# Block inverse by interleaved independent streams on VectorE, and GpSimd limited to one-input operations, in a DeltaNet and Soft-MoE kernel

**Chip, cores, metric.** One core of a Trainium2 chip. The time is the device time of a run in microseconds (us). Ratios are the mean time of one kernel's fast runs over that of the kernel before in the same rounds, so not quite the ratio of the medians that stand beside them. Below, PE is TensorE, DVE VectorE, ACT ScalarE, POOL GpSimd, SP SyncE.

## The reference, cut to what matters

```python
def _attn_ref(q, k, v, beta):                 # (4, 8, 768, 48) each; beta (4, 8, 768)
    k_n = k / (np.linalg.norm(k, axis=-1, keepdims=True) + 1e-06)
    for t in range(S):
        y[:, :, t] = einsum(q_t, state)
        v_old = einsum(state, k_n_t)
        state = state + beta_t * outer(k_n_t, v_t - v_old)
# x = y as (3072, 384); logits = x @ phi (32 slots); softmax over tokens -> slot_input = d.T @ x
# 8 experts: relu(slot_input @ w1) @ w2; softmax over slots -> out = c @ slot_out
```

The kernel works in 24 chunks of 32 tokens, six groups of four. In a chunk the recurrence becomes a product with the inverse of a triangular 32x32 matrix for each of the 32 (batch, head) pairs. The 128 inverses of a group's four chunks are computed at once, one per partition.

## The kernel before

While group n runs, VectorE eliminates the inverses of group n+1, a few steps at a time, in program order between its other work. Each step is a product and then a subtraction of that product:

```python
        def eliminate(j):                                   # 31 of them per group
            m, w = j + 1, C - 1 - j
            ...
            nc.vector.tensor_tensor(prv, tt[:, j, 0:m]..., lb[:, j, j + 1:C]..., op=ALU.mult)
            nc.vector.tensor_tensor(tt[:, j + 1:C, 0:m], tt[:, j + 1:C, 0:m], prv, op=ALU.subtract)
```

GpSimd does three two-input products per chunk on 128 partitions (and the scalings of `lb` and of the inverse):

```python
    def scale_v(cc):
        nc.gpsimd.tensor_tensor(Vt[cc], Vt[cc], nT[n][...].broadcast_to([P, U, D]), op=ALU.mult)
    def weights(cc):
        nc.gpsimd.tensor_tensor(Ab[cc % NT], wide(GQ[n][:, c, :, :, 1, :]...), tri..., op=ALU.mult)
        nc.gpsimd.tensor_tensor(Tb[cc % NT], wide(TT[n][:, c * U:(c + 1) * U, :]), own..., op=ALU.mult)
```

The dependence that matters: `R = V - K S` is a VectorE operation, and TensorE's solve (`T R`, 32 products) waits for it:

```python
        def rest():
            state(0, ks)                                    # TensorE: K S into PSUM
            nc.vector.tensor_tensor(R, Vt.pop(cc), ks, op=ALU.subtract)
        def solve():                                        # 32 matmuls: lhsT=T[y][:, u], rhs=R
        ...
        # order in a chunk
        hook("head"); drain(EL[c][0]); rest(); read(); scale_v(x + 2); ...; drain(EL[c][1])
        solve(); turn(...); ...; drain(EL[c][2]); update(); outputs(); ...; weights(x + 1)
```

`EL[c][p]` are the elimination steps of the next group that are put at place p of chunk c. The group's norms and the scaling of `lb` stand at place 0 of its first chunk, ahead of R.

## Time and profile before

| | before |
|---|---|
| time, median of 3 | 401.38 us |
| profiled span, granted TensorE clock | 398.2 us, 0.843 |
| first solve; groups 0 to 4, solve to solve | 48.9; 54.0, 47.7, 48.6, 45.5, 46.2 us |
| last group and the experts (from solve 20 to the end) | 107.3 us |
| solve idle for R | 31.7 us in 16 waits |

"Solve to solve" is the distance between the first matmuls of two solves in TensorE's timeline. As each chunk needs the state that the one before left, these distances add up to the time of the loop.

### The profile page before, as it was taken

What the parts mean: (1) busy time and instruction counts of PE and PEld (TensorE: products, weight loads), DVE (VectorE), ACT (ScalarE), POOL (GpSimd) and SP (SyncE); (2) the same over time, 40 slices, a digit from 0 to 9 for tenths busy, and PEclk for the clock granted to TensorE, in tenths of its full rate; (3) what the DMA queues carried; (4) which work ended last, traced back from release to release, by engine and by line L of the source; (5) the groups of instructions that cost most, each with busy time, mean ns of one, the idle gap of its engine ahead of it and who ended that gap; (6) DMA issues with size and microseconds to landing.
All of it is one profiled execution on the core that took longest, in us unless ns stands there. A gap on an engine that the chain in (4) does not pass through costs nothing.

```text
span 398.2 us, 16603 instructions
## 1 busy us (share of the span) xinstructions
PE 310.5 (78%) x7391; PEld 247.8 (62%) x7391; DVE 235.4 (59%) x554; ACT 147.8 (37%) x296; POOL 120.5 (30%) x144
## 2 busy tenths in 40 slices
PE   3676869789939897699986898396998968866784
PEld 2555757677938786578775787385986854312243
DVE  6396499651887968689687987979412022101043
ACT  2343223465514564235542463232535521101032
POOL 9320442440504535063350826134352000000000
PEclk9999975996865899758998689856799978999685
DMA  5555445544422245424311011011400499799148
GB/s 96 92 96 82 76 79 86 87 77 67 78 47 38 40 76 113 92 48 98 54 23 22 11 30 29 2 21 21 162 3 4 172 425 426 283 431 428 56 172 302
DMA packets 85031, 45.27 MB, mean 114 GB/s; under 512 B 79424, under 2 KB 82656, under 8 KB 83040
## 3 DMA queue, kind: packets, MB, share of 16 engines
q1 hardware_dynamic: 83296, 43.86, 40.7%
q8 instruction: 58, 0.95, 1.0%
q0 software_dynamic: 576, 0.15, 0.3%
q10 hardware_dynamic: 1088, 0.20, 0.3%
q14 instruction: 13, 0.11, 0.1%
HBM read 39.47 MB, written 4.72 MB: 111 GB/s over the span
## 4 chain that ended last, share of the span: by engine, by line
PE 34%; DVE 26%; SPq 12%; issue 11%; DMA 9%; ACT 3%; POOL 3%; DVEq 0%; POOLq 0%; ACTq 0%
SPq L82 11%; DVE pr L320 10%; DVE tt L323 8%; DMA w2t<-in_moe_w_dram 5%; PE psR L434 5%; PE psS L447 3%; PE pso L879 3%; PE pt L482 3%; PE pt L585 3%; PE pt L211 3%; PE psY L464 3%; DVE R L427 2%; PE psR L420 2%; PE ph L855 2%; PE pt L567 2%
## 5 line engine op out<-in xcount | busy, mean ns | idle before, releaser
L320 DVE TENSOR_TENSOR pr<-tt,lb 128x31 f32<-128x31 f32 (+15 forms) x155 | 76.0, 490 | 7.2 <-POOL lb L312 2.9
L323 DVE TENSOR_TENSOR tt<-tt,pr 128x31 f32<-128x31 f32 (+15 forms) x155 | 70.0, 452 | 5.3
L434 PE MATMUL psR<-R,Tb 64*64 64x48 f32 x768 | 31.4, 238 | 31.7 <-DVE R L427 31.7
L434 PEld LDWEIGHTS psR<-R,Tb 64*64 64x64 f32 x768 | 28.7, 153 | 35.1 <-issue 24.1
L454 ACT ACTIVATE S<-psS 48x768 f32<-48x768 f32 x46 | 37.1, 806 | 30.2 <-PE psS L447 29.9
L312 POOL TENSOR_TENSOR tt<-tt,gm 128x512 f32<-128x512 f32 x10 | 11.4, 1136 | 101.7 <-DVE pr L320 64.8
L396 POOL TENSOR_TENSOR Tb<-TT,own 128x512 f32<-128x512 f32 x24 | 26.4, 1102 | 30.0 <-ACT TT L376 25.3
L240 PE MATMUL pt<-KQ 48*32 48x64 f32 (+1 forms) x1792 | 27.7, 248 | 7.2 <-ACT KQ L227 4.7
L393 POOL TENSOR_TENSOR Ab<-GQ,tri 128x512 f32<-128x512 f32 x24 | 32.1, 1336 | 4.0 <-ACT GQ L244 4.0
L437 ACT ACTIVATE U<-psR 128x384 f32<-128x384 f32 x24 | 11.8, 492 | 57.8 <-PE psR L434 57.8
L464 PE MATMUL psY<-U,Ab 64*64 64x48 f32 x768 | 32.5, 243 | 0.0
L447 PE MATMUL psS<-U,K 32*112 32x96 f32 x736 | 31.1, 321 | 0.7 <-ACT U L437 0.6
L240 PEld LDWEIGHTS pt<-KQ 48*32 48x32 f32 x1792 | 22.4, 124 | 14.4 <-ACT KQ L227 6.1
L464 PEld LDWEIGHTS psY<-U,Ab 64*64 64x64 f32 x768 | 29.2, 157 | 3.0 <-issue 1.2
L244 ACT ACTIVATE GQ<-pt 128x256 f32<-128x256 f32 (+1 forms) x56 | 16.8, 351 | 37.5 <-PE pt L240 37.5
L447 PEld LDWEIGHTS psS<-U,K 32*112 32x112 f32 x736 | 26.8, 223 | 5.5 <-ACT U L437 1.9
L420 PE MATMUL psR<-S,KQ 128*32 128x96 f32 x768 | 26.2, 288 | 1.6 <-issue 1.1
L420 PE MATMUL psY<-S,KQ 128*32 128x96 f32 x768 | 25.2, 283 | 0.0
L385 POOL TENSOR_TENSOR V<-V,nT 128x384 f32<-128x384 f32 x24 | 21.6, 901 | 11.4 <-DMA Q<-in_q_dram 7.5
L269 DVE STREAM_TRANSPOSE lb<-GQ 128x1024 f32<-128x1024 f32 x6 | 11.8, 1968 | 21.0 <-ACT GQ L244 21.0
L211 PE MATMUL pt<-ident,Q 128*128 128x128 f32 x76 | 23.1, 341 | 1.3 <-DMA Q<-in_q_dram 0.9
L420 PEld LDWEIGHTS psR<-S,KQ 128*32 128x32 f32 x768 | 20.3, 129 | 3.8 <-issue 2.1
(143 smaller groups left out, 498.8 us busy)
## 6 DMA issues: line engine op xcount, KB each, us to landing
w2t<-in_moe_w_dram SPq DMA_DIRECT2D x8, 1536.0 KB, 19.0
w1t<-in_moe_w_dram SPq DMA_DIRECT2D x7, 1536.0 KB, 10.6
Q<-in_q_dram SPq DMA_DIRECT2D x96, 48.0 KB, 2.8
V<-in_v_dram SPq DMA_DIRECT2D x96, 48.0 KB, 2.8
out_dram<-ob SPq DMA_DIRECT2D x24, 192.0 KB, 2.4
K<-in_k_dram SPq DMA_DIRECT2D x92, 48.0 KB, 2.5
w1t<-in_moe_w_dram SPq DMA_DIRECT2D x3, 512.0 KB, 4.0
bb<-in_beta_dram POOLq DMA_DIRECT2D x16, 6.0 KB, 2.7
```

The source lines that it names most:

```text
L82: eng.dma_start(out=dst[C * h:C * h + C, :, 0:D], in_=src.rearrange("b (g h) s d -> h s (b g) d", h=4)[h, cc * C:(cc + 1) * C])
L211: nc.tensor.transpose(dst, self.src[a][:, b * G:(b + 1) * G, :].rearrange("p g d -> p (g d)"), ident)
L240: nc.tensor.matmul(pg[g][rh, b], lhsT=kq[r, b, 0, rh], rhs=kq[r, b, a0:a1, rh], start=True, stop=True, skip_group_check=True)
L320: nc.vector.tensor_tensor(prv, tt[:, j, 0:m].unsqueeze(1).broadcast_to([P, w, m]), lb[:, j, j + 1:C].unsqueeze(2).broadcast_to([P, w, m]), ...
L323: nc.vector.tensor_tensor(tt[:, j + 1:C, 0:m], tt[:, j + 1:C, 0:m], prv, op=ALU.subtract)
L393: nc.gpsimd.tensor_tensor(Ab[cc % NT], wide(GQ[n][:, c, :, :, 1, :].rearrange("p b g t -> p (b g) t")), tri.unsqueeze(1).broadcast_to([P, ...
L396: nc.gpsimd.tensor_tensor(Tb[cc % NT], wide(TT[n][:, c * U:(c + 1) * U, :]), own.unsqueeze(1).unsqueeze(3).broadcast_to([P, U, 2, C]), op= ...
L420: nc.tensor.matmul(dst[hs[h], b].rearrange("p g d -> p (g d)"), lhsT=kq[:, b, a, hs[h]], rhs=old[:, h, b, :], start=(b == 0), stop=False, ...
L434: nc.tensor.matmul(pw[half[y], u], lhsT=T[y][:, u], rhs=st["R"][half[y], u], start=(u == 0), stop=True, skip_group_check=True)
L447: nc.tensor.matmul(psS[0:DP + D, h, b * GD:(b + 1) * GD], lhsT=K[hs[h], b * G:(b + 1) * G].rearrange("p g d -> p (g d)")[:, 0:DP + D], rhs ...
L454: nc.scalar.activation(new[r, :, :, g * D:(g + 1) * D], psS[r, :, 0:B * GD].rearrange("p h (b g e) -> p h b g e", b=B, g=G)[:, :, :, g], A ...
L464: nc.tensor.matmul(qs[half[y], b, g], lhsT=at[y][:, u], rhs=st["U"][half[y], u], start=False, stop=True, skip_group_check=True)
```

## The change

Its intent: (1) split the inverse into diagonal blocks (E), a coupling with the lower left block (M) and a combination (L), and interleave their steps so that an operation seldom needs the result of the one directly ahead; (2) no operation on GpSimd with two SBUF inputs, since they hold VectorE's two-input steps (in the profile before, 31 elements took 1.02 us beside such a product, 112 took 0.27 without); (3) the first group's inverse likewise, without TensorE.

```diff
+            for j in range(HC):                      # HC = 16
+                put(..., ea(j)); put(..., ma(j))     # products of streams E and M
+                put(..., es(j)); put(..., ms(j))     # their subtractions
+            for j in range(HC + 1):
+                if j < HC: put(..., la(j))           # products of the combination ...
+                if j > 0:  put(..., ls(j - 1))       # ... one ahead of the sums
     def scale_v(cc):
-        nc.gpsimd.tensor_tensor(Vt[cc], Vt[cc], nT[n]...broadcast_to([P, U, D]), op=ALU.mult)
+        for u in range(U):                           # 8 pieces 128x48
+            nc.gpsimd.tensor_scalar(Vt[cc][:, u], Vt[cc][:, u], nT[n][:, ...], None, op0=ALU.mult)
     def weights(cc):
-        nc.gpsimd.tensor_tensor(Ab[cc % NT], wide(GQ...), tri..., op=ALU.mult)
-        nc.gpsimd.tensor_tensor(Tb[cc % NT], wide(TT...), own..., op=ALU.mult)
+        for h in range(4):                           # 4 pieces 32x256
+            nc.gpsimd.affine_select(out=Ab[...][r, :, h % 2, :], in_=GQ[n][r, c, :, :, 1, :], ...)
+        for h in range(4):                           # 4 pieces 32x256
+            nc.gpsimd.tensor_copy(Tb[...][r, :, h % 2, :], TT[n][r, c * U:(c + 1) * U, :])
-    # scaling of lb, of the inverse, and Call: GpSimd
+    # scaling of lb, of the inverse, and Call: VectorE
-    f0["couple"](0); f0["combine"](0); ...           # first group: half inverse, rest on TensorE
+    drain([t[1] for t in f0["steps"]])               # first group: the same 95 steps
```

The table of what is prepared in chunks 0 to 3 changes with it. The shares of the steps per place stay: .29, .30, .26 and .15 of them in chunks 0 to 3 of a group.

## The prediction

> **What bounds the kernel now.** I read the engines' busy shares, then the chain that ended last, then the timeline of each engine inside one group of four chunks (144 to 194 us), and last busy time by stretch. By shares TensorE leads (78%), VectorE has 59%. The costliest groups say more:
>
> ```profile
> L320 DVE TENSOR_TENSOR pr<-tt,lb 128x31 f32<-128x31 f32 (+15 forms) x155 | 76.0, 490 | 7.2 <-POOL lb L312 2.9
> L323 DVE TENSOR_TENSOR tt<-tt,pr 128x31 f32<-128x31 f32 (+15 forms) x155 | 70.0, 452 | 5.3
> L434 PE MATMUL psR<-R,Tb 64*64 64x48 f32 x768 | 31.4, 238 | 31.7 <-DVE R L427 31.7
> ```
>
> 146 us of VectorE are the elimination of five inverses, and the solve L434 sat idle 31.7 us, all for R, which stands behind elimination steps in VectorE's queue. TensorE in the timeline:
>
> ```profile
> 160.86 0.86 PE L240 MATMUL pt<-KQ 48*32 48x64 f32 x64
> 164.87 1.94 PE L434 MATMUL psR<-R,Tb 64*64 64x48 f32 x32 [3.16 <-DVE R L427]
> ...
> 189.59 1.14 PE L434 MATMUL psR<-R,Tb 64*64 64x48 f32 x32
> ```
>
> After a wait of 3.16 us the same 32 products take 1.94 us instead of 1.14: the wait is paid twice. VectorE then:
>
> ```profile
> 151.14 1.02 DVE L320 TENSOR_TENSOR pr<-tt,lb 128x31 f32<-128x31 f32 x1 [0.59 <-POOL lb L312]
> 152.19 0.77 DVE L323 TENSOR_TENSOR tt<-tt,pr 128x31 f32<-128x31 f32 x1
> ...
> 156.34 0.27 DVE L320 TENSOR_TENSOR pr<-tt,lb 128x112 f32<-128x112 f32 x1
> 156.64 0.28 DVE L323 TENSOR_TENSOR tt<-tt,pr 128x112 f32<-128x112 f32 x1
> ...
> 163.84 0.42 DVE L323 TENSOR_TENSOR tt<-tt,pr 128x247 f32<-128x247 f32 x1
> 164.18 0.55 DVE L427 TENSOR_TENSOR R<-V,psR 128x384 f32<-128x384 f32 x1
> 164.64 0.41 DVE L320 TENSOR_TENSOR pr<-tt,lb 128x252 f32<-128x252 f32 x1
> ...
> 179.49 0.54 DVE L427 TENSOR_TENSOR R<-V,psR 128x384 f32<-128x384 f32 x1
> 179.95 0.77 DVE L320 TENSOR_TENSOR pr<-tt,lb 128x231 f32<-128x231 f32 x1
> 180.75 0.40 DVE L323 TENSOR_TENSOR tt<-tt,pr 128x231 f32<-128x231 f32 x1
> ```
>
> and POOL beside it:
>
> ```profile
> 150.05 2.06 POOL L312 TENSOR_TENSOR lb<-lb,gm 128x512 f32<-128x512 f32 x2 [3.33 <-DVE gm L295]
> 152.07 0.83 POOL L385 TENSOR_TENSOR V<-V,nT 128x384 f32<-128x384 f32 x1
> ...
> 179.26 1.20 POOL L396 TENSOR_TENSOR Tb<-TT,own 128x512 f32<-128x512 f32 x1
> 180.41 0.97 POOL L263 MEMSET tt<- 128x1056 f32 x1
> ```
>
> Three things. 31 elements take 1.02 us beside a POOL product, 112 take 0.27 without: a blocked step ends with the POOL operation. A POOL memset blocks nothing (231 elements, 0.40), nor does POOL hold R (0.54 at 179.49), which has one input in SBUF. And the next step starts 0.30 us after a step of 112 that it depends on, but R starts 0.34 after one of 247 that it doesn't. By stretches (columns: length, busy us of PE, PEld, DVE, ACT, POOL, then the granted clock):
>
> ```profile
> 103.00:151.00 48.00, 39.16 (x1039) 34.52 (x1038) 38.56 (x87) 22.82 (x45) 19.31 (x20) 0.79 0.32 54
> 151.00:199.00 48.00, 40.39 (x1055) 35.19 (x1050) 38.70 (x89) 21.97 (x43) 18.43 (x20) 0.82 0.40 80
> ```
>
> So groups 1 to 4 (48, 48, 46, 46 us) are VectorE's: 38.6 us busy of 48, nearly all the rest its waits in order for TensorE (2.6 for a transposed maximum, 2.3 for slot products and so on). TensorE's 39 us are busy at a clock of 0.8. The tail, some 107 us from solve 20 (290.93) to the end, is four light chunks and then weight transfers (TensorE waits for w2 up to 371.7).
>
> [...]247 elements at 1.04 ns (231 against 112 elements, 0.40 against 0.275) are 257 ns, R starts 340 after; from R (384, 400 ns) to the next step 460. I use n x 1.04 + 60 ns. Dependent steps measure n x 1.04 + 195.
> [...]no line shows POOL with one input beside such a step. The change bets that this doesn't block[...].
> [...]
>
> **The change part by part.**
> (1) Elimination of one group, n>=1. Before: 62 dependent steps, 10,912 elements: 62 x 0.195 + 11.4 = 23.5 us, plus blocking: 146/5 = 29.2 us measured busy against 62 x 0.165 + 11.4 = 21.6 unblocked, so 7.6. About 31 us in all. After: 95 steps, 11,936 elements (diagonal blocks 2720, coupling 2 x 2176, combination 2 x 2176, scaling 512): 95 x 0.06 + 12.4 = 18.1 us if nothing depends. I laid the steps out with 60/195: the first small ones still wait. And by the built program each step of the combination's product waits for the sum just ahead of it (they share tile tt, in other columns), so the second stream is not independent: some 14 x 0.125 us. Sum 20.6.
> (2) Moved to VectorE: scaling of lb, 768 elements in two operations, 1.05 us and now ahead of R of a group's first chunk (before it was 2.06 on POOL after it, with 0.59 of VectorE waiting); Call, 0.25.
> (3) POOL per chunk: 3 operations (0.83 + 1.27 + 1.04) become 16 small ones. By the 4-element affine_select of the start (about 0.2 us) and a memset's rate (1056 in 0.97), estimates: 8 x 0.17 + 4 x 0.38 + 4 x 0.36 = 4.3 us one after the other[...]. It fits in a chunk.
> (4) First group: 30 + 3 operations and 512 small products with two copies become the 95 steps. Its inverse starts at 20.2 us as before: 20.2 + 1.1 + 20.6 + 0.5 blocking + 1.9 for two transposes = 44.3, then Tb, spread, norms and lb ahead of R(0) (two transposes and norms took 10.2 us from 37.8, with 4.6 of waiting): R about 50.3, solve 0 at 51 instead of 48.9. Loss 2. Against it the products leave chunks 0 to 3, with idle "issue" gaps of 2.67 and 1.13 us.
>
> **Laid out by chunk**, uncontended, TensorE with its warm durations, VectorE in its order (the shares of the steps as in the code, each summed with 60/195). TensorE's warm work from solve to solve is solve 1.1, turn 0.5, transposes 0.9, update 1.0, outputs 1.1, state products 1.4, next products 0.8 and 1.0 to 2.4 of routing: 8 to 9 us, 34 a group. Where VectorE is later than that, R sets the next solve. Solve to solve:
> first chunk: 2.7 us of steps, wait to 4.1 for the slot products, 2.8 of steps, wait to 8.0 for the logits, 1.9 of steps, R: 10.8 (was 14.2);
> second: 1.8, waits and small ones to 3.5, 1.9, shares to 6.5, 1.7, R: 8.9 (was 15.2);
> third: VectorE 7.0 before R: 7.8 (was 9.4);
> fourth: the norms can't start before 6.5, norms 1.9, lb 1.05, R: 10.3 (was 9.0).
> Group: 37.8 instead of 48. No wait of TensorE is over 2 us[...]. The last such group has no spread: 34. Chunks 0 to 3 (no routing, but SyncE's issues at 0.49 us each): 39 instead of 54. Solve 20 then falls at 51 + 39 + 3 x 37.8 + 34 = 237 instead of 291; with the unchanged 107 us the span is 345, and 348 as timed (401.4 timed to 398.2).
>
> **The rivals.** A: one-input POOL operations don't block: 348. For it: the author's pains[...]. B: they block in full and run one after the other: 4 x 4.3 = 17 us of POOL reads per group, as many as before (V 3.3, Ab 4.9, Tb 4.2, scalings 4.2, Call 0.4), of which 7.6 were lost; again 7 to 8 lost, groups of 45, about 377.[...] C: they block, but [...]only hold short operations: 3 us per group, 361. D: the gain is not to be had, since TensorE or SyncE becomes the bound (34 us of warm products per group; 12 issues of 0.49 a chunk, 6 us): near 385. Against it: solve 7 to 8 took 9.0 us with hardly any wait. E: weight transfers hide it. Against it: the second weight load waits for the last R, so the tail moves with the loop.
>
> **Range and chances.** A 0.5, C 0.25, B 0.15, D and unforeseen 0.1. The middle of these is about 356 us; range 341 to 382. Faster by over 2%: 0.94; within: 0.04; slower: 0.02.
>
> **What would show it.** Right: elimination near 20 to 21 us a group and no step of 16 to 60 elements above 0.3 us; L434's waits for R under 12 us in all; granted clock about 0.95 between 90 and 240 us; solve 0 near 51; tail of about 107. Combination products spaced by 0.195, coupling ones by 0.06. Wrong: steps still stretched beside POOL (B, C), solve waiting for Tb or V from POOL, or low clock in spite of short waits.

## The result

| | before | after | predicted |
|---|---|---|---|
| time, median | 401.46 us (4 runs) | 376.31 us (4 runs, 374.76 to 378.55) | 356 (341 to 382) |
| ratio | | 0.939, 95% interval 0.932 to 0.946 | |
| profiled span, granted clock | 398.2, 0.843 | 376.8, 0.898 | 345 if nothing blocks |
| first solve | 48.9 | 51.8 | 51 |
| groups 0 to 4 | 54.0, 47.7, 48.6, 45.5, 46.2 | 43.3, 43.0, 46.0, 43.7, 39.6 | 39, 37.8, 37.8, 37.8, 34 |
| from solve 20 to the end | 107.3 | 109.4 | 107 |

Faster by 6%, inside the range, but 20 us above the predicted point: 25 us won instead of 45. From the page of the changed kernel, the costliest groups (busy us, mean ns of one, then idle time ahead of them and what ended it):

```profile
L371 POOL TENSOR_SCALAR V<-V,nT 128x48 f32<-128x48 f32 x192 | 87.5, 479 | 9.5 <-DMA Q<-in_q_dram 7.3
L385 POOL COPY Tb<-TT 32x256 f32<-32x256 f32 x96 | 42.7, 444 | 68.0 <-DVE TT L362 45.8
L421 PE MATMUL psR<-R,Tb 64*64 64x48 f32 x768 | 30.7, 235 | 32.3 <-DVE R L414 24.6
L379 POOL TENSOR_SCALAR_AFFINE_SELECT Ab<-GQ 32x256 f32<-32x256 f32 x96 | 50.1, 522 | 3.6
...
L297 DVE TENSOR_TENSOR prM<-tt,lb 128x16 f32<-128x16 f32 (+7 forms) x96 | 31.3, 326 | 0.0
L302 DVE TENSOR_TENSOR nm<-nm,prM 128x16 f32<-128x16 f32 (+7 forms) x96 | 30.4, 317 | 0.0
```

Solve still sits idle for 32.3 us, as long as before (31.7). The profile puts 24.6 of them down to R and 7.8 to the elimination product `prE`, which ends right behind R in VectorE's queue, so these are waits for R too:

```profile
94.48 0.50 DVE L414 TENSOR_TENSOR R<-V,psR 128x384 f32<-128x384 f32 x1
94.91 0.17 DVE L297 TENSOR_TENSOR prE<-tt,lb 128x30 f32<-128x30 f32 x1
...
95.14 1.71 PE L421 MATMUL psR<-R,Tb 64*64 64x48 f32 x32 [2.76 <-DVE prE L297]
```

GpSimd needs 180 us for V, Ab and Tb (87.5 + 42.7 + 50.1), 7.5 us per chunk: the small pieces cost 0.44 to 0.52 us each, one after the other. (VectorE's busy sums are not to be compared with those of before: the records of independent steps overlap, a step of 128 lasting 0.28 us with the next started after 0.20.)

VectorE's timeline in the first chunk, with GpSimd's below it, shows the first loss:

```profile
55.30 0.28 DVE L297 TENSOR_TENSOR prE<-tt,lb 128x126 f32<-128x126 f32 x1
55.50 0.50 DVE L297 TENSOR_TENSOR prM<-tt,lb 128x112 f32<-128x112 f32 x1
55.93 0.28 DVE L302 TENSOR_TENSOR tt<-tt,prE 128x126 f32<-128x126 f32 x1
56.13 0.50 DVE L302 TENSOR_TENSOR nm<-nm,prM 128x112 f32<-128x112 f32 x1
```

```profile
51.67 3.71 POOL L371 TENSOR_SCALAR V<-V,nT 128x48 f32<-128x48 f32 x8
55.33 2.46 POOL L379 TENSOR_SCALAR_AFFINE_SELECT Ab<-GQ 32x256 f32<-32x256 f32 x4
```

Beside the selects every other step takes 0.50 us instead of 0.27 (112 elements took 0.27 in the profile of before). Before 55.3, beside the V pieces, the steps are as short as they should be: at 55.11 one of 96 elements took 0.27. So one-input GpSimd operations do hold VectorE, but not all of them.

TensorE's timeline at the start of group 2 shows the second:

```profile
138.13 1.14 PE L421 MATMUL psR<-R,Tb 64*64 64x48 f32 x32 [2.32 <-DVE R L414]
139.20 0.64 PE L469 MATMUL pt<-ident,Y 128*96 128x128 f32 x4
139.68 0.27 PE L192 MATMUL pt<-ident,K 128*128 128x128 f32 x1
139.79 0.38 PE L192 MATMUL pt<-ident,Q 128*128 128x128 f32 x1
139.96 0.42 PE L192 MATMUL pt<-ident,K 128*128 128x128 f32 x1
140.18 0.42 PE L192 MATMUL pt<-ident,Q 128*128 128x128 f32 x1
140.53 2.84 PE L572 MATMUL pt<-Y,dr 64*64 64x97 f32 x32
```

After a wait of 2.32 us the solve runs at full pace, but 1.8 us later the transposes go from 0.27 to 0.42 us and the slot products take 2.84 us (1.55 elsewhere). The next VectorE work waits for these slot products, and R stands behind it.

### The profile page after: what moved, and what is told of

Same layout as the page of the kernel before. It is cut to its first block, busy times and chain, and to the rows that moved or that the text cites.

```text
span 376.8 us, 16124 instructions
## 1 busy us (share of the span) xinstructions
PE 292.9 (78%) x6879; PEld 229.9 (61%) x6879; DVE 239.5 (64%) x801; ACT 145.4 (39%) x292; POOL 199.5 (53%) x434
## 4 chain that ended last, share of the span: by engine, by line
PE 50%; DVE 14%; DMA 11%; SPq 10%; ACT 7%; issue 5%; POOL 1%; DVEq 0%; ACTq 0%; POOLq 0%
SPq L82 9%; PE psR L421 8%; PE psS L434 7%; DMA w2t<-in_moe_w_dram 6%; PE pt L572 6%; PE psY L451 5%; PE pt L192 5%; PE pt L469 4%; PE pso L864 4%; ACT S L441 3%; DMA Q<-in_q_dram 3%; DVE R L414 2%; PE pt L221 2%; PE psR L407 2%; PE ph L840 2%
## 5 line engine op out<-in xcount | busy, mean ns | idle before, releaser
L371 POOL TENSOR_SCALAR V<-V,nT 128x48 f32<-128x48 f32 x192 | 87.5, 479 | 9.5 <-DMA Q<-in_q_dram 7.3
L385 POOL COPY Tb<-TT 32x256 f32<-32x256 f32 x96 | 42.7, 444 | 68.0 <-DVE TT L362 45.8
L421 PE MATMUL psR<-R,Tb 64*64 64x48 f32 x768 | 30.7, 235 | 32.3 <-DVE R L414 24.6
L379 POOL TENSOR_SCALAR_AFFINE_SELECT Ab<-GQ 32x256 f32<-32x256 f32 x96 | 50.1, 522 | 3.6
L421 PEld LDWEIGHTS psR<-R,Tb 64*64 64x64 f32 x768 | 28.0, 149 | 35.9 <-issue 24.9
L297 DVE TENSOR_TENSOR prL<-tt,nm 128x256 f32<-128x256 f32 (+7 forms) x96 | 30.3, 320 | 2.8
L297 DVE TENSOR_TENSOR prM<-tt,lb 128x16 f32<-128x16 f32 (+7 forms) x96 | 31.3, 326 | 0.0
L302 DVE TENSOR_TENSOR nm<-nm,prM 128x16 f32<-128x16 f32 (+7 forms) x96 | 30.4, 317 | 0.0
L302 DVE TENSOR_TENSOR tt<-tt,prL 128x256 f32<-128x256 f32 (+7 forms) x96 | 29.5, 307 | 0.2
L297 DVE TENSOR_TENSOR prE<-tt,lb 128x30 f32<-128x30 f32 (+7 forms) x90 | 29.3, 326 | 0.0
L302 DVE TENSOR_TENSOR tt<-tt,prE 128x30 f32<-128x30 f32 (+7 forms) x90 | 29.2, 324 | 0.0
L434 PE MATMUL psS<-U,K 32*112 32x96 f32 x736 | 27.9, 297 | 0.1
L434 PEld LDWEIGHTS psS<-U,K 32*112 32x112 f32 x736 | 23.8, 200 | 4.8 <-issue 1.8
L572 PE MATMUL pt<-Y,dr 64*64 64x97 f32 x384 | 22.3, 277 | 1.4 <-ACT dr L563 1.4
```

The costliest lines, as they stand in the source:

```text
L297: nc.vector.tensor_tensor(pr, a.broadcast_to([P] + shape), b.broadcast_to([P] + shape), op=ALU.mult)
L302: nc.vector.tensor_tensor(dst, dst, pr, op=op)
L371: nc.gpsimd.tensor_scalar(Vt[cc][:, u], Vt[cc][:, u], nT[n][:, c * U + u:c * U + u + 1], None, op0=ALU.mult)
L379: nc.gpsimd.affine_select(out=Ab[cc % NT][r, :, h % 2, :].rearrange("p (b g) t -> p b g t", g=G), in_=GQ[n][r, c, :, :, 1, :], compare_op= ...
L385: nc.gpsimd.tensor_copy(Tb[cc % NT][r, :, h % 2, :], TT[n][r, c * U:(c + 1) * U, :])
L421: nc.tensor.matmul(pw[half[y], u], lhsT=T[y][:, u], rhs=st["R"][half[y], u], start=(u == 0), stop=True, skip_group_check=True)
```

## The experiments

The theory: what is missing was lost in two places, (a) VectorE's steps stretched beside GpSimd's selects and copies, (b) a lower TensorE clock after waits of 2 to 3 us. The rivals: the combination's false dependence, GpSimd's lateness, or VectorE's order of work, which would leave the time where it is even with (a) and (b) gone. A further question is what each part of the change is worth.

How "stretched" is counted below: from VectorE's timeline between 18 and 300 us, a step of n elements is stretched if its duration exceeds 0.150 us + 1.04 ns x n by over 0.12 us. The excesses are summed.

| run | median us | ratio to before (95%) | stretched steps, mean excess, sum | solve idle, all (of it put down to R), us |
|---|---|---|---|---|
| before | 401 to 404 | 1 | 59 x 0.71 = 42 us | 31.7 (31.7) |
| after | 376.31 | 0.939 (0.932 to 0.946) | 104 x 0.21 = 22 us | 32.3 (24.6) |
| streams_alone | 400.73 | 0.994 (0.987 to 1.001) | 60 x 0.77 = 46 us | 42.5 (42.5) |
| pool_alone | 387.48 | 0.964 (0.958 to 0.970) | 77 x 0.17 = 13 us | 26.7 (18.5) |
| v_product | 387.32 | 0.963 (0.959 to 0.968) | 106 x 0.27 = 29 us | 39.8 (36.9) |
| serial | 405.05 | 1.005 (0.998 to 1.011) | 101 x 0.19 = 19 us | 49.2 (36.9) |
| tb_act | 384.21 | 0.953 (0.947 to 0.960) | 33 x 0.22 = 7 us | 33.7 (24.9) |
| l_split | 380.77 | 0.944 (0.938 to 0.951) | 99 x 0.21 = 21 us | 32.6 (19.6) |
| weights_memset (wrong result) | 371.44 | 0.916 (0.907 to 0.925) | 0 | 28.1 (16.4) |
| warm | 370.55 | 0.919 (0.912 to 0.925) | 102 x 0.21 = 22 us | 18.3 (13.1) |
| warm_memset (wrong result) | 364.41 | 0.903 (0.897 to 0.910) | 0 | 14.9 (9.3) |
| late_norms | 366.75 | 0.910 (0.903 to 0.918) | 85 x 0.21 = 18 us | 22.8 (14.8) |
| late_norms_warm | 366.11 | 0.908 (0.902 to 0.913) | 86 x 0.21 = 18 us | 14.2 (10.0) |

The experiments came in four sessions and the result in another, so compare ratios, not medians. In `warm`, `warm_memset` and `late_norms_warm` idle products fill part of the wait, so their idle time is lower by construction. Results were correct but for the two marked ones, and for the measurement below.

### What holds VectorE, measured by itself

```diff
+    for name, f, count in kinds:                     # 13 kinds of GpSimd operation
+        for i in range(count): f(i)                  # GpSimd: count operations, Y <- X
+        for i in range(20):                          # VectorE: 40 dependent steps ...
+            nc.vector.tensor_tensor(pr[0], tt[0], lb, op=ALU.mult)
+            nc.vector.tensor_tensor(tt[0], tt[0], pr[0], op=ALU.subtract)
+        for i in range(20):                          # ... and 40 independent ones, 128x128 all
+            nc.vector.tensor_tensor(pr[1], tt[1], lb, op=ALU.mult)
+            nc.vector.tensor_tensor(pr[0], tt[0], lb, op=ALU.mult)
```

> Wrong result on purpose: a measurement of one thing. VectorE runs 20 pairs of dependent two-input steps (128 elements) and then 40 independent products of 128 elements, 13 times, each time beside another run of GpSimd operations. Alone: a dependent step about 0.30 us to the next, an independent one about 0.20. Beside the two-input product 128x512: one step per product, about 1 us. Beside a memset: as alone. Theory by size[...]: tensor_scalar 128x384 and 32x256 stretch steps as copies and selects of 256 do, and copy and select of 48 elements do not. Theory by kind: copies and selects stretch steps at every size, tensor_scalar at none. Theory of partitions: the 32-partition forms stretch and the 128-partition forms do not.

VectorE's timeline beside the two-input product, beside copies of 256 elements, beside a tensor_scalar of 384 (independent steps), and beside copies of 48:

```profile
57.29 8.86 POOL L85 TENSOR_TENSOR Y<-X 128x512 f32<-128x512 f32 x8 [13.54 <-DVE Y L126]
57.38 1.09 DVE L131 TENSOR_TENSOR tt<-tt,pr 128x128 f32<-128x128 f32 x1
58.51 1.08 DVE L130 TENSOR_TENSOR pr<-tt,lb 128x128 f32<-128x128 f32 x1
...
88.12 0.42 DVE L131 TENSOR_TENSOR tt<-tt,pr 128x128 f32<-128x128 f32 x1
88.58 0.41 DVE L130 TENSOR_TENSOR pr<-tt,lb 128x128 f32<-128x128 f32 x1
89.03 0.41 DVE L131 TENSOR_TENSOR tt<-tt,pr 128x128 f32<-128x128 f32 x1
...
231.25 0.59 DVE L133 TENSOR_TENSOR pr<-tt,lb 128x128 f32<-128x128 f32 x1
231.75 0.28 DVE L134 TENSOR_TENSOR pr<-tt,lb 128x128 f32<-128x128 f32 x1
...
232.76 0.58 DVE L133 TENSOR_TENSOR pr<-tt,lb 128x128 f32<-128x128 f32 x1
...
267.63 0.29 DVE L130 TENSOR_TENSOR pr<-tt,lb 128x128 f32<-128x128 f32 x1
267.95 0.29 DVE L131 TENSOR_TENSOR tt<-tt,pr 128x128 f32<-128x128 f32 x1
```

The mean distance between the starts of dependent steps, while GpSimd is busy:

| beside | one GpSimd operation, mean us | step to step, us |
|---|---|---|
| nothing | | 0.327 (independent: 0.202) |
| memset 32x256 | 0.30 | 0.327 |
| two-input product 128x512 | 1.04 | 1.12 |
| copy 32x256; 128x256 | 0.39; 0.40 | 0.45; 0.46 |
| affine_select 32x256; 128x256 | 0.39; 0.40 | 0.46; 0.47 |
| copy 128x48; affine_select 128x48 | 0.26; 0.25 | 0.33; 0.33 |
| tensor_scalar 128x48 (scale from SBUF; constant) | 0.51; 0.38 | 0.34; 0.34 |
| tensor_scalar 32x256; 128x384 (scale from SBUF) | 1.06; 1.34 | 0.37; 0.40 |

Copies, selects and the two-input product of 256 elements or more alternate with VectorE: one step for each GpSimd operation, each step about as long as the operation. At 48 elements nothing of it shows in dependent steps; copies and selects of 48 met no independent ones here. The number of partitions plays no part, which rules out the theory of partitions.

A tensor_scalar, too, stretches one step for each operation. Beside it the independent steps, 0.20 us apart otherwise, are 0.23 us apart once per operation of 48 elements, 0.40 at 256 and 0.51 at 384 (231.25 to 231.75 above). So what one operation holds grows with its size: 0.03, 0.20 and 0.31 us. That is the theory by size. The kind shows in how often this happens: a copy of 256 came every 0.45 us, a tensor_scalar of 384 every 1.43.

### GpSimd's part alone, the streams alone

`pool_alone` is the kernel before with the new `scale_v` and `weights` and with the scalings and Call on VectorE. `streams_alone` is the changed kernel with these taken back.

```diff
 # pool_alone, against the kernel before
-        nc.gpsimd.tensor_tensor(Vt..., / Ab..., / Tb...)      # and lb, inverse, Call on GpSimd
+        8 tensor_scalar, 4 affine_select, 4 tensor_copy        # and lb, inverse, Call on VectorE
 # streams_alone, against the changed kernel: the reverse (lb of groups 1 to 5 and Call on GpSimd)
```

> The kernel before with the new GpSimd operations alone (V, Ab, Tb in pieces with one input; scalings of lb and of the inverse and Call moved to VectorE); elimination and first group as before. If one-input operations relieve VectorE: 7.6 us of stretching less per group against about 2.5 us of scalings added, so some 380. If they block about as much as two-input ones: 400 to 412.

> The changed kernel with GpSimd's old two-input operations (V, Ab, Tb, scaling of lb in groups 1 to 5, Call); streams and first group as changed. If one-input operations on GpSimd gave the gain, this gives most of it back: 390 or more. If the streams alone gave it and the new GpSimd operations block about as much as the old ones: 372 to 382, within 2% of the changed kernel.

The streams alone gain nothing that the interval shows (0.994), GpSimd's part alone 3.6%, both together 6.1%. But `streams_alone` also has the new first group, and `pool_alone` the old one. By stages of the profiled runs (us):

| run | to the first solve | group 0 | groups 1 to 4 | from solve 20 on |
|---|---|---|---|---|
| before | 48.9 | 54.0 | 188.0 | 107.3 |
| pool_alone | 49.2 | 54.5 | 171.6 | 109.6 |
| streams_alone | 52.8 | 47.9 | 184.7 | 109.3 |
| serial (below) | 57.2 | 46.1 | 190.6 | 108.6 |
| after | 51.8 | 43.3 | 172.3 | 109.4 |

In groups 1 to 4 `pool_alone`, with the old elimination of 62 dependent steps, is as fast as the changed kernel. So there GpSimd's part gives the whole gain, and no gain of the interleaved streams over the old elimination shows. What the changed kernel has beyond `pool_alone` lies in group 0. There solve waits for R in neither of them in chunks 1 to 3; `pool_alone` runs 324 products more on TensorE (1404 against 1080, 256 of them the first inverse's), at a granted clock of 0.78 instead of 1.00:

```profile
55.34 1.79 PE L364 MATMUL pt<-dr,GQ 16*32 16x16 f32 x119
70.43 1.26 PE L376 MATMUL pt<-TT,dr 32*32 32x16 f32 x128
```

That points to the first group's inverse without TensorE, part (3), and the reordered preparation. A run with parts (2) and (3) and the old elimination would settle it and was not made.

VectorE and then GpSimd at the start of group 1 of `streams_alone`:

```profile
102.84 1.29 DVE L307 TENSOR_TENSOR prM<-tt,lb 128x16 f32<-128x16 f32 x1
104.05 1.12 DVE L312 TENSOR_TENSOR tt<-tt,prE 128x30 f32<-128x30 f32 x1
105.07 0.86 DVE L312 TENSOR_TENSOR nm<-nm,prM 128x16 f32<-128x16 f32 x1
...
108.22 0.18 DVE L312 TENSOR_TENSOR nm<-nm,prM 128x32 f32<-128x32 f32 x1
```

```profile
102.83 1.27 POOL L388 TENSOR_TENSOR Ab<-GQ,tri 128x512 f32<-128x512 f32 x1
104.05 1.05 POOL L391 TENSOR_TENSOR Tb<-TT,own 128x512 f32<-128x512 f32 x1
105.05 0.84 POOL L380 TENSOR_TENSOR V<-V,nT 128x384 f32<-128x384 f32 x1
```

16 elements take 1.29 us, as long as the GpSimd product beside them; 32 take 0.18 as soon as GpSimd is done. What is lost goes by the number and length of GpSimd's operations, not by the number of VectorE's steps: 60 stretched steps and 46 us here, 59 and 42 us before, with 95 steps per group instead of 62. So short steps keep all of the loss, and here it sits ahead of R of the groups' second chunks (first intervals 15.2 to 15.3 us); solve's waits for R rose from 31.7 to 42.5 us. That the streams' closer spacing didn't show at all in spite of it is read from these waits, not isolated further.

### The order of the steps; V in pieces

```diff
 # serial: the same 95 steps, each product directly ahead of its sum
+            for j in range(HC - 1): put(..., ea(j)); put(..., es(j))
+            for j in range(HC):     put(..., ma(j)); put(..., ms(j))
+            ... scale ...
+            for j in range(HC):     put(..., la(j)); put(..., ls(j))
 # v_product: the changed kernel, V scaled by one two-input product of 128x384 as before
```

> The changed kernel with the same 95 steps in the order of the mathematics (each product directly followed by its sum) instead of interleaved. If interleaving hides the dependent spacing (0.325 against 0.202 us, as measured with steps of 128): about 60 steps more wait 0.12 us, 7 us per group, 40 us in all before TensorE hides any: 400 to 415. If it matters little: under 385.

> The changed kernel with V scaled by one two-input product of 128x384 on GpSimd per chunk, as before, instead of eight one-input pieces of 128x48 (3.8 us of GpSimd, which stretch hardly any step). If splitting V is a gain of its own, each product holds one or two steps by 0.6 us or more: stretching rises from 22 to some 40 us, time 380 to 386. If GpSimd's lateness with the eight pieces costs as much as they save: within 1%, 373 to 380.

Without the interleaving the same operations take 405.05 us: all of the gain is gone (29 us by the medians, 26 by the ratios 0.939 and 1.005). So a chain cut into 95 steps needs the interleaving; that it then beats the uncut chain is not shown, since `pool_alone` took the same time for groups 1 to 4. With V as one product, 2.4 points of the ratio are lost, more than the first expectation's upper figure (387 against 380 to 386), though stretching rose only from 22 to 29 us; 39.8 instead of 32.3 us of idle time ahead of solve show where most of it went. The eight pieces are a good bargain in spite of their 3.8 us on GpSimd.

### The missing 20 us: contention and clock

```diff
 # weights_memset: Ab and Tb written by memsets of the same shapes (wrong result)
-            nc.gpsimd.affine_select(out=Ab[...], in_=GQ..., ...)
+            nc.gpsimd.memset(Ab[cc % NT][r, :, h % 2, :], 0.0)
-            nc.gpsimd.tensor_copy(Tb[...], TT...)
+            nc.gpsimd.memset(Tb[cc % NT][r, :, h % 2, :], 0.0)
 # warm: TensorE kept busy while it waits for R
         def solve():
+            for _ in range((4, 4, 2, 0)[c] if n < NG - 1 else 0):
+                nc.tensor.matmul(psY[:, 384:512], lhsT=ident, rhs=ident, start=False, stop=True, ...)
 # warm_memset: both
```

> Wrong result on purpose: the changed kernel with Ab and Tb written by memsets of the same shapes, which read nothing. If copies and selects stretching VectorE's steps cost most of the missing 20 us: 355 to 362. If the rest is TensorE's low clock and VectorE's waits in order: 370 or more.

> The changed kernel with 4, 4, 2, 0 idle products of TensorE (128x128 by 128 columns into an unused part of a PSUM bank, read by nobody) placed ahead of the solve of the first, second, third, fourth chunk of groups 0 to 4, so that TensorE isn't idle while it waits for R. Theory of the lower clock (what is missing beside the stretched steps is paid by TensorE after its waits, and by what waits for TensorE then: slot products 2.7 to 2.8 us instead of 1.55, transposes 0.42 instead of 0.27): 10 us less, about 366, and a granted clock near 0.98 from 90 to 260 us. Rival (the waits in order would be the same with a warm TensorE): within 1% of the changed kernel, 372 to 380, or above it, by the products themselves.

> Wrong result on purpose: the changed kernel with both the memsets for Ab and Tb and the idle products ahead of the solves, so with no stretched steps and a TensorE that stays at full clock. If stretching and lower clock are all that the prediction's layout of a group left out: 346 to 352, groups of 37.8. If each counts for itself but something third remains: 356 to 361. If the two losses are the same waits seen twice: 364 to 370, no better than one of them.

`weights_memset`: no step is stretched any more, and the ratio falls from 0.939 to 0.916, some 9 us of 401.5. That rests on two runs; with the two slow ones it would be 0.921 and 7 us. The memsets are also shorter than copies and selects (0.30 us) and read no inverse, so GpSimd is done earlier; but in the changed kernel only 0.5 us of R's idle time is put down to GpSimd's V, and nothing of the idle time of solve's products to V, Ab or Tb (waits of its weight loads are: 9.8 us for V and 6.5 for Tb). `warm`: 0.919, some 8 us, with as many stretched steps as before. TensorE's timeline of `warm` at the same place as above:

```profile
136.00 1.16 PE L419 MATMUL psY<-ident 128*128 128x128 f32 x8
137.79 1.14 PE L424 MATMUL psR<-R,Tb 64*64 64x48 f32 x32 [0.64 <-DVE prE L297]
...
139.66 0.27 PE L192 MATMUL pt<-ident,Q 128*128 128x128 f32 x1
140.18 1.55 PE L575 MATMUL pt<-Y,dr 64*64 64x97 f32 x32 [0.24 <-ACT yT L473]
```

The four idle products (eight records) fill 1.16 us of the wait; the transposes stay at 0.27 and the slot products take 1.55 instead of 2.84. By stretches (length, busy us of PE, PEld, DVE, ACT, POOL, then the granted clock), from 90 to 260 us of the changed kernel and of `warm`:

```profile
90.00:260.00 170.00, 139.79 (x3772) 122.87 (x3772) 142.24 (x485) 78.98 (x155) 126.64 (x266) 0.86 0.31 60
```

```profile
90.00:260.00 170.00, 150.56 (x4156) 132.52 (x4155) 145.68 (x499) 83.45 (x163) 138.57 (x286) 0.94 0.31 61
```

The clock goes from 0.86 to 0.94 (0.98 was expected). Both together give 0.903, 14 us less than the changed kernel, not the 17 of the sum: the shorter waits of one also spare some of the other's loss. Its groups are 44.4, 37.8, 41.2, 39.9, 34.1 us. One of them meets the predicted 37.8, the last meets 34.

### Other suspects

```diff
 # l_split: la reads a copy of the scaled lower right block (one more step), no false dependence
+                lr = st["lr"] = wk.tile([P, HC, HC], ...)
+                nc.vector.tensor_tensor(lr, tt[:, HC:C, HC:C], gm..., op=ALU.mult)
 # tb_act: Tb on ScalarE
-            nc.gpsimd.tensor_copy(Tb[...][r, :, h % 2, :], TT[n][r, ...])      # 4 of them
+            nc.scalar.activation(Tb[cc % NT][:, :, x, :], TT[n][...], ACT.Identity, scale=own[:, x:x + 1])
```

> The changed kernel with a copy of the scaled lower right block in a tile of its own, which the combination's products read; so they no longer wait for the sum ahead of them, at the price of one more step of 256 elements. By the spacing (0.44 instead of 0.31 us on 14 steps, 1.75 us, less 0.33) the steps of a group take 1.4 us less; all six inverses are ahead of a solve: up to 8 us less, 368 to 371. If these steps lie in time that VectorE waits for TensorE anyway: no change.

> The changed kernel with Tb made by two scaled activations of 128x256 on ScalarE instead of four copies of 32x256 on GpSimd. Correct result. GpSimd loses 1.8 us per chunk, VectorE's steps are stretched by selects alone, some 12 instead of 22 us in all. If what the stretching costs is what counts: 4 to 6 us less, 370 to 373. If ScalarE's 0.9 us more per chunk delay TensorE's next operands: 377 or more.

`l_split` (0.944, interval overlapping that of the changed kernel) shows no gain; that the combination lies in the third and fourth chunk, whose ends wait for other things, may be why. `tb_act` is slower (0.953), though only a third of the stretching is left. Why is not shown: in the profiled runs it is 4.4 us longer, of which 4.3 lie in group 0, and there TensorE waits 3.8 us for a load of Q that it doesn't wait for in the changed kernel. The weight loads of solve waited for ScalarE's Tb as well (3.7 us by the view of its line). So this run doesn't tell what fewer stretched steps are worth.

### A version that beats both

The changed kernel does the norms and the scaling of `lb` for the next group ahead of R of a group's first chunk, which doesn't need them.

```diff
-        at[0][0] += [f["norms"]]
+        at[0][1] += [f["norms"]]                     # behind R
-    share = [(0.0, 0.14, 0.15), (0.10, 0.10, 0.10), (0.09, 0.09, 0.08), (0.10, 0.05, 0.0)]
+    share = [(0.0, 0.10, 0.09), (0.06, 0.10, 0.09), (0.08, 0.12, 0.10), (0.10, 0.13, 0.0)]
```

> The changed kernel with the norms and the scaling of lb moved behind R of a group's first chunk (they have nothing to do with that R) and the shares of the steps moved from the first two chunks to the last two. If R's place in VectorE's queue is what makes the first chunks long: the interval ahead of a group's first solve falls from 11 to 12 us to about 9, the others stay near 10 to 11, groups of 39 to 41, time 355 to 368. If VectorE's total work per group is the bound already: no change, 372 to 380.

> The same with 3, 3, 2, 0 idle products ahead of the solves. If waits over 2 us remain: 4 to 8 us below the run without them. If the waits are short now: the same or up to 3 us above.

`late_norms`, 366.75 us with a correct result, is 3 points of the ratio better than the changed kernel (0.910 against 0.939). The first solve falls to 49.3, and the intervals ahead of the solves of chunks 8, 12 and 16 from 11.0, 11.6 and 9.1 us to 8.4, 8.7 and 8.6; groups 1 to 4 take 39.6, 40.4, 39.7 and 40.4, though group 0 takes 46.5 instead of 43.3: at 69.8 TensorE has waited 7.04 us for a load of Q, so the loads of group 0 are one more place to look. The idle products add nothing that the intervals show (0.908). Of the 22.8 us that TensorE was idle ahead of solve in `late_norms`, 14.8 are put down to R, but 4.1 and 3.4 now to GpSimd's V and Tb: its 7.5 us per chunk are a candidate for the next limit.

## Why the prediction was right in range and 20 us off in size

**Right.** The bound (VectorE's queue ahead of R), the direction, the first solve (51.8 for 51), GpSimd's memset as harmless (steps 0.327 us apart beside it and alone), the spacing of the combination's steps: in the changed kernel they start alternately 0.31 and 0.44 us apart (164.83, 165.14, 165.58). So was, nearly, the sum of 20.6 us for the steps of one inverse: VectorE is busy with them, overlaps counted once, for 21.1 us per inverse in `weights_memset`, and for 25.1 in the changed kernel, where copies and selects stretch them.

**The gain, part by part.** The layout took a group's gain from blocking (7.6 us) and from the shorter steps (23.5 to 20.6 us). The second part doesn't show: groups 1 to 4 take 172.3 us with the streams and 171.6 without (`pool_alone`). `serial` shows that the 95 steps need the interleaving, not that they beat the 62. So the direction was right, and the predicted credit for the streams was not.

**"A 0.5: one-input POOL operations don't block."** This failed in part. V's eight pieces of 48 elements hardly do (dependent steps 0.34 us apart in `ports`, 0.327 alone), copies and selects of 256 do, one step for each (0.45 to 0.47 us). That is rival C, "only hold short operations": 3 us per group were estimated, 22 us in six inverses (3.7 each) measured. On the time it was worth some 9 us (`weights_memset`). Rival B, full blocking as before, was wrong by half: 22 against 42 us. The prediction's own sign, no step of 16 to 60 elements above 0.3 us, failed as well: 18 were, up to 0.49. No line of the profile before could tell A from C; but C's price of 361 us was too low, because of the next two steps. (Weighted by the prediction's chances, its four prices give 359 us, not 356.)

**"No wait of TensorE is over 2 us."** This failed, and with it the granted clock of about 0.95. That waits under 2 us would leave TensorE at its warm durations was the estimate. The profile before shows solves of 1.13 to 1.24 us after waits of 0.17 to 2.46 us and of 1.94 or 1.95 after 3.16 to 6.61, but also one of 1.94 after 0.29 us. In the changed kernel waits of 1.9 to 2.8 us remained in the first two chunks of groups 1 to 4, of 2.9 and 3.3 us in the third of groups 1 and 4, and the lower clock after them cost some 8 us (`warm`). The clock between 90 and 260 us was 0.86, not 0.95. The argument was circular: the waits were short in a layout that assumed a warm TensorE and unstretched steps.

**The layout by chunk.** With stretching and most of the clock's loss taken out (`warm_memset`; its profiled run is the fastest of four, 4 us below the median), the span is 358.7 us, against 344.4 by the layout's own terms (51 + 39 + 3 x 37.8 + 34 + 107). Of the 14.3 us, group 0 has 5.4 (44.4 for 39), groups 1 to 3 together 5.5 (37.8 + 41.2 + 39.9 for 113.4), the tail 3.1 (110.1 for 107). In group 0 the interval from chunk 3 to 4 measures 12.3 us here and in the changed kernel; the trace of the changed kernel shows why: the spread of `lb` waits 2.46 us for products of chunk 11, the norms then 1.47 us for ScalarE. With them behind R it is 9.5 us (`late_norms`, which moves the steps' shares too). So that part is put down to R's place behind them, a wait in order that the layout had priced too low. Inside a later group the layout held for the first and the fourth chunk (10.8 and 10.3 us in group 2, as predicted), but not for the second and third: 10.7 instead of 8.9, and 9.4 instead of 7.8 us. In the second the small operations of the routing end later than laid out (the shares 8.5 us after R instead of 6.5, in VectorE's timeline of `weights_memset`). Why the tail is 2 to 3 us longer was not settled.

**GpSimd per chunk.** 4.3 us were estimated from a 4-element select and a memset's rate; 7.5 were measured. The pieces don't overlap (from 51.67 us eight of V take 3.71 us, then four selects 2.46 and four copies 2.22), and a tensor_scalar of 48 elements costs 0.48. It fitted into a chunk as predicted; what the miss cost was not measured by itself.

**"L434's waits for R under 12 us."** 32.3 us were measured, with those put down to `prE`; with both losses gone the group lengths come near the layout. The miss of the sum is thus 9 us stretching and 8 us clock (14 together), and the layout's own misses for the rest.

## What to carry to other kernels

Split a gain by stages before crediting a part of a change: together the parts gave 6.1%, GpSimd's alone 3.6% and the rest 0.6%, which looks as if the streams paid once GpSimd no longer held them; but in groups 1 to 4 the streams added nothing to GpSimd's part, and the rest of the gain lay in group 0. Cutting a VectorE chain into more steps without interleaving them cost all of the gain. What mattered beside GpSimd was the size and the kind of GpSimd's operation (dependent steps of 128 elements 0.45 us apart beside copies of 256, 0.33 beside copies of 48, 0.40 beside a tensor_scalar of 384), so measure the very form. Before a chain is moved off an engine that gates a solve, look at what else stands ahead of the gating operation without need: moving the norms behind R, and the steps' shares with them, was worth half as much as the whole change. And do not assume a full clock in a layout: between 90 and 260 us it was 0.86 here, and waits of 2 to 3 us on TensorE cost another 8 us in what followed them (`warm`).

## What the runs show of GpSimd beside VectorE and of the clock

- VectorE's two-input steps of 128 elements beside GpSimd (`ports`): copies and selects of 256 elements per partition hold one step for one operation (0.45 to 0.47 us from step to step instead of 0.327), a memset none (0.327). Copies and selects of 48 elements show no hold beside dependent steps (0.33). A tensor_scalar holds one step per operation, by 0.03 us at 48 elements, 0.20 at 256 and 0.31 at 384, though the operations last 0.51, 1.06 and 1.34 us.
- Four GpSimd operations on 32 different partitions each did not overlap: 0.44 us (copy) and 0.52 us (affine_select) each in the changed kernel, one after the other, and in `ports` a copy took 0.39 us on 32 and 0.40 on 128 partitions. Memsets of 32 partitions did not overlap either: 0.30 us each, 0.36 from start to start.
- A small GpSimd operation by kind, beside a busy VectorE (`ports`): copy 0.26 us at 48 and 0.39 at 256 elements, tensor_scalar with its scale in SBUF 0.51 at 48 and 1.34 at 384.
- The clock: waits of 2.2 to 3.3 us ahead of solve came before a lower pace, which could begin 1.8 us after work had resumed (0.27 to 0.42 us per transpose at the start of group 2). In the changed kernel's trace all changes of the granted clock lie whole multiples of 3.41 us apart (95.45, 98.86, 119.34, 122.75, 139.82, 143.23 and so on). Between 90 and 260 us the stretches of 3.41 us that the half clock followed had 1.6 to 2.8 us of idle time, as from 136.41 to 139.82, where TensorE was busy for 1.69 of 3.41 us (columns as above):

```profile
136.41:139.82 3.41, 1.69 (x38) 1.66 (x39) 3.41 (x13) 0.63 (x2) 3.12 (x8) 1.00 0.41 69
139.82:143.23 3.41, 3.41 (x37) 2.92 (x35) 2.29 (x12) 1.19 (x2) 3.27 (x9) 0.50 0.60 166
```

After one stretch with 1.9 us (235.40 to 238.81) the clock stayed at 1.00, so the exact measure stays open.
- Independent VectorE steps of 128 elements start 0.202 us apart (`ports`): 0.133 at 1.04 ns per element (the profile before: 231 against 112 elements, 0.40 against 0.275 us), and 0.069 beside. Dependent steps start 0.12 us later (0.327).
